# Attention with sinks and two MLPs on one core: another order of the attention pairs' steps in the opening stretch

## The chip, the cores and the metric

The kernel runs on one core of a Trainium2 chip. The metric is the device time of one execution in microseconds (us), taken as the median of several runs. The core has a matrix engine (TensorE, PE in the profile; its weight loads are PEld), VectorE (DVE), ScalarE (ACT), GpSimd (POOL) and SyncE (SP), whose queue issues the transfers from and to memory (DMA). Each engine executes its own instructions strictly in the order of the program, and waits for other engines by semaphores.

## The reference

Attention over 2 batches x 8 heads x 768 positions of 64 elements, where each position sees the last 128 positions and the first 4 (the sinks), and two MLPs one behind the other on the result (1536 tokens x 512, with 2048 inner features). All inputs are fp32.

```
scores = scale * q @ k.T
keep = (pos < n_sink) | ((rel >= 0) & (rel < window))
scores = where(keep, scores, -1e9);  scores -= max(scores)
a = exp(scores);  a = a / (sum(a) + 1e-9)
x = (a @ v)                                  # heads side by side: 1536 x 512
h = x @ w_in;   g = max(h, 0) + alpha * min(h, 0);   x = g @ w_out
h = x @ w2_in;  g = h - tanh(h);                     out = g @ w2_out
```

The weights are handed over as 64-bit numbers and converted to fp32 on the chip.

## The kernel before

**Pairs.** The attention is cut into 48 *pairs* of heads: a unit u is a batch and a block of 128 queries (12 units), and each unit has four pairs p; the pair's number is n = 4u + p. Two pairs share a *group* G = n // 2 of keys and queries. From the second block of a batch on, a pair's scores are 128 x 288 for each of its two heads (own block, previous block and 32 sink columns); in the first block they are 128 x 128.

**Steps of a pair.** `s_mm` (L244, L250): the scores on TensorE. From unit 1 on, keys and queries are split in a high and a low part, kept in `kq`, and three products (high-high, low-high, high-low) are added. `kq_hi` (L214, ScalarE) makes a group's high part, `kq_lo` (L217, VectorE) the low part as the difference, and `k_sinks` (L223) copies sink columns. `s_max` (L259, VectorE, an instruction and a short read of the accumulator for each head): mask and row maximum. `s_exp` (L268, ScalarE): exponential and its sum. `norm_sum` (L274 adds 1e-9 to the sums, L276 takes reciprocals) and `norm` (L283, one instruction per head), all VectorE. `sink_copy` (L292, VectorE, every second pair) gathers the sink columns. `t_mm` (L302, TensorE): transposes; `sink_mm` (L324) those of the sink columns. `t_ev` (L309) and `sink_ev` (L328) copy them out on ScalarE. `pv` (L341, L342, and L345 for sinks, TensorE): products with v. After every fourth pair `x_h` (L352, ScalarE) and `x_l` (L357, VectorE) store the unit's result as high and low part, the input of the first MLP.

**Stages.** The opening stretch is the loop of L531: 19 turns (`S_LEAD`), n = 0 to 18, one pair a turn, in which steps of neighbouring pairs are interleaved by hand: turn n makes the scores of pair n + 1, the maxima and exponentials of pair n, the norms and transposes of pair n - 1 and the products with v of pair n - 2. It also converts the first two weight tiles (L52 on ScalarE, then L54, L56, L58 and L60 on VectorE, one instruction a turn), splits one (L195, L200) and writes the masks (L488). The main loop (L621) then has 96 steps (2 MLPs x 3 token blocks x 16 feature tiles) of h products (L370), activation and output products (L422). Its first 29 pairs' worth of steps carry the remaining attention pairs, and its first 14 the rest of the first MLP's weight conversion.

**What sets the order.** The kernel is scheduled by hand: each engine's order is the order in which the code calls the steps. The order within one engine alone counts; that two calls for different engines change places has no effect. Loads of keys and queries (`load_qk`) are issued from SP four groups ahead, into six buffers.

Of the kernel before, what the change touches and what calls it, by code (L numbers as in the profile page):

```python
# [21 lines left out]
S_LEAD = 19  # L22
# [3 lines left out]
NU = B * NB  # L26
# [94 lines left out]
def fast_path(tc, qk, v, vsink, limits, w1i, w1o, alpha, w2i, w2o, out, outer):  # L121
# [3 lines left out]
    with ExitStack() as ctx:  # L125
# [79 lines left out]
        initial = [True]  # L205
# [7 lines left out]
        def kq_hi(G):  # L213
            nc.scalar.activation(out=kq_part(G, 0), in_=raws[G].rearrange("p c e t -> p c (e t)"), func=AF.Copy)  # L214

        def kq_lo(G):
            nc.vector.tensor_tensor(kq_part(G, 1), raws[G].rearrange("p c e t -> p c (e t)"), kq_part(G, 0), op=ALU.subtract)  # L217
# [60 lines left out]
        def norm(n):  # L278
            u, p, b, i, w = geom(n)
            G, hh = 2 * u + p // 2, 2 * (p % 2)  # L280
            for a in range(2):
                e = pq[G][:, hh + a, 0:w]
                nc.vector.tensor_scalar(e, e, sums[G][:, hh + a:hh + a + 1], None, op0=ALU.mult)  # L283
            if not initial[0]:
                sink_copy(n)

        def sink_copy(n):
            u, p, b, i, w = geom(n)
            G = 2 * u + p // 2
            if p % 2 == 1 and i >= 2:  # L290
                sks[G] = ap.tile([128, 4, SINK], F32, name="sk", bufs=1)
                nc.vector.tensor_copy(sks[G], pq[G][:, :, 128:160])  # L292
# [215 lines left out]
            if n == 4 * NB + 4:  # L508
                load_vs(1)

        def splits(n):

            todo = {0: (0,), 1: (2,), 2: (1,)}.get(n, (n // 2 + 2,) if n % 2 == 1 else ())
            for G in todo:
                if G < 2 * NU:
                    kq_hi(G)
                    kq_lo(G)
                    if G // 2 in (0, NB):
                        k_sinks(G)
# [11 lines left out]
        for n in range(S_LEAD):  # L531
            last = n == S_LEAD - 1
            a_loads(n)
            if n == 0:
                s_mm(0)
            if n >= 2:
                t_ev(n - 2)
            if not last:
                s_mm(n + 1)
            if n >= 1:  # L540
                norm_sum(n - 1, 0)
            s_max(n, 0)
            s_exp(n, 0)
            if n >= 1:
                norm_sum(n - 1, 1)
            s_max(n, 1)
            s_exp(n, 1)
            if n >= 2 and has_sinks(n - 2):
                sink_ev(n - 2)
            if n >= 5 and n % 4 == 2:  # L550
                x_l(n - 3)
            if n == 0:
                masks(0)
            if n >= 1:
                norm(n - 1)
            if n >= 2 and not last:
                pv(n - 2)
            if n >= 5 and n % 4 == 1:
                x_h(n - 2)
            splits(n)  # L560
            if n == 2:
                masks(1)
            if n == 3:
                load_w(0, 1)
            for f, at in CONV0:
                if n == at:
                    conv_start(0, f)
                if at < n < at + 5:
                    conv_step(0, f)
                if n == at + 4:  # L570
                    load_w(0, f + 2)
                if n == at + 6 and f == 0:
                    split_w(0, 0, 0, 0)
                    split_lo(0, 0, 0, 0)
            if n >= 1:
                sink_copy(n - 1)
                if not last:
                    t_mm(n - 1)
                    if has_sinks(n - 1):
                        sink_mm(n - 1, n + 1)  # L580
        initial[0] = False
        conv_start(0, len(CONV0))

# [37 lines left out]
        for g in range(N):  # L621
            m, c, f = steps[g]
            n = S_LEAD + g
            att = n < NPAIR + 3
            att_s = att and n < NPAIR
            back = steps[g - 1] if g else None
            first = g < NF
            conv = ahead = load = None
            L = len(CONV0)
            if first and g + L < NF:  # L630
                conv, ahead = (0, g + L), (0, g + L + 1) if g + L + 1 < NF else None
                load = (0, g + L + 2) if g + L + 2 < NF else None
            if g == CONV1 - 2:
                stage[1] = [ap.tile([128, 2048], I32, name="raw2", tag="kq", bufs=2) for _ in range(2)]
                load_w(1, 0)
                load_w(1, 1)
            if g == CONV1 - 1:
                ahead = (1, 0)
            conv1 = start.get(g, slow.get(g - 3))
            slow1 = next((slow[t] for t in range(g - 3, g + 1) if t in slow), None)  # L640
            if g in start:
                conv = (1, start[g])
            if g + 1 in start or g + 1 in slow:
                ahead = (1, start.get(g + 1, slow.get(g + 1)))
            if conv1 is not None and conv1 + 2 < NF:
                load = (1, conv1 + 2)
            if g == 2 * NF + 1:
                flag()
            if g == 2 * NF + 3:
                flag_rest()  # L650

            if att and n - 2 < NPAIR:
                t_mm(n - 2)
                t_ev(n - 2)
                if has_sinks(n - 2):
                    sink_mm(n - 2, n)
                    sink_ev(n - 2)
            if m == 0:
                if g + 1 < N:
                    split_w(*steps[g + 1], 0)  # L660
                if back:
                    split_w(*back, 1)
                if att_s:
                    a_loads(n)
                if att and n - 1 < NPAIR:
                    norm_sum(n - 1, 0)
                    norm_sum(n - 1, 1)
                    norm(n - 1)
                if conv:
                    conv_step(*conv)  # L670
                h_mm(m, c, f, 0, 2)
                if att_s:
                    s_mm(n)
                    for a in range(2):
                        s_max(n, a)
                        s_exp(n, a)
                h_mm(m, c, f, 2, 4)
                if back:
                    evac_mid(*back)
                    evac_hi(*back)  # L680
                    split_lo(*back, 1)
                if g + 1 < N:
                    split_lo(*steps[g + 1], 0)
                evac_first(m, c, f)
                if back:
                    evac_lo(*back)
                if conv:
                    conv_step(*conv, 3)
                if ahead:
                    conv_start(*ahead)  # L690
            elif m == 1:
                if back[0] == 0:
                    evac_mid(*back)
                    evac_hi(*back)
                    split_w(*back, 1)
                    split_lo(*back, 1)
                    evac_lo(*back)
                    split_w(*steps[g + 1], 0)
                    split_lo(*steps[g + 1], 0)
                if g != N - 1:  # L700
                    h_mm(m, c, f, 0, 4)
                if g == N - 2:
                    h_mm(*steps[g + 1], 0, 4)
                if g == N - 1:
                    out_mm(*steps[g - 3], 0, 4)
                if g < N - 2:
                    out_mm(*steps[g - 2], 0, 4)
                evac_first(m, c, f)
                if steps[g - 2][2] == NF - 1:
                    out_ev(*steps[g - 2][:2])  # L710
                evac_mid(m, c, f)
                if g + 2 < N:
                    split_w(*steps[g + 2], 0)
                split_w(m, c, f, 1)
                evac_hi(m, c, f)
                if g + 2 < N:
                    split_lo(*steps[g + 2], 0)
                split_lo(m, c, f, 1)
                evac_lo(m, c, f)
                if slow1 is not None:  # L720
                    conv_step(1, slow1)
                if ahead:
                    conv_start(*ahead)
            if m == 0 and g >= 2:
                out_mm(*steps[g - 2], 0, 4)
                if steps[g - 2][2] == NF - 1:
                    out_ev(*steps[g - 2][:2])
            if att:
                pv(n - 3)
                if n % 4 == 2:  # L730
                    x_h(n - 3)
                    x_l(n - 3)
                splits(n)
            if load:
                load_w(*load)
        for t in steps[N - 3:]:
# [179 lines left out]
```

## Time and profile before

| | |
|---|---|
| median of 3 runs | 702.11 us (701.14 to 704.3) |
| profiled execution | 701.61 us, its span 699.8 us |
| mean granted TensorE clock over the span | 0.981 of full speed |
| busy in the span: TensorE, VectorE, ScalarE | 655.1, 564.1, 433.3 us |
| busy tenths in the first five of 40 slices (17.5 us each) | TensorE 4 9 7 6 9, VectorE 5 6 7 7 8 |

The span is the time from the first to the last instruction; the profiled execution's own time is 1.8 us longer. Busy times are sums over one engine, idle times are given with what ended them ("releaser"), and the source line of each instruction is that of the kernel before. A matmul's end in the profile is modelled, so TensorE's rows are read best by their starts.

### The profile page before, as it was taken

To read this page: it belongs to the slowest core of one execution; us is meant where nothing else is said; L and a number is where in the kernel's file an instruction comes from. 1 tells how busy PE (TensorE), PEld (TensorE's weight loads), DVE (VectorE), ACT (ScalarE), POOL (GpSimd) and SP (SyncE) were. 2 spreads that over 40 slices of the span, in tenths; PEclk is the share of its full clock that TensorE was granted. 3 is DMA by queue.
4 is the path that set the end of the run, shared out by engine and by line. 5 is a ranking of instruction groups with operands and counts; after the bars stand their busy time and mean duration, and the time that the engine had idled before them with its cause. 6 is when DMAs were issued, how large, how long until landed. Compare 5 with 4: busy or idle time off the path is not lost.

```text
span 699.8 us, 9115 instructions
## 1 busy us (share of the span) xinstructions
PE 655.1 (94%) x3194; PEld 504.9 (72%) x3194; DVE 564.1 (81%) x1159; ACT 433.3 (62%) x872; POOL 1.1 (0%) x8
## 2 busy tenths in 40 slices
PE   4976989999999999999899999999999999999985
PEld 3654667766777777777688887777777777778763
DVE  5677899999967656658999987999888887887873
ACT  4756666657566565544646557777776777766653
POOL 0000000000000000000000000000000000000000
PEclk9987999999999999999999999999999999999999
DMA  3733244555010000113334330100010000100001
GB/s 107 225 116 111 76 142 153 183 169 170 12 46 2 15 16 1 59 64 120 121 125 170 127 121 1 60 1 0 1 60 1 1 0 1 60 1 1 0 1 65
DMA packets 27030, 47.35 MB, mean 68 GB/s; under 512 B 3168, under 2 KB 15456, under 8 KB 26976
## 3 DMA queue, kind: packets, MB, share of 16 engines
q1 hardware_dynamic: 26976, 46.68, 19.5%
q8 instruction: 27, 0.44, 0.3%
q14 instruction: 27, 0.22, 0.1%
HBM read 43.53 MB, written 3.15 MB: 67 GB/s over the span
## 4 chain that ended last, share of the span: by engine, by line
DVE 38%; PE 34%; ACT 20%; issue 4%; SPq 3%; DMA 1%; DVEq 0%; ACTq 0%
PE ps_h L370 13%; PE ps_o L422 13%; DVE u L106 5%; DVE g L109 4%; DVE g L108 4%; DVE t L107 4%; ACT mask L101 4%; ACT b L100 4%; ACT gh L401 4%; DVE wf L58 3%; ACT t L99 3%; ACT u L98 3%; DVE wl L200 3%; SPq L161 2%; DVE gl L406 2%
## 5 line engine op out<-in xcount | busy, mean ns | idle before, releaser
L370 PE MATMUL ps_h<-x,wh 128*128 128x512 f32 x384 | 127.6, 413 | 5.1 <-ACT t L377 3.6
L200 DVE TENSOR_TENSOR wl<-wf,wh 128x512 fp32r<-128x512 f32 x192 | 123.4, 683 | 10.7 <-ACT wh L195 10.5
L195 ACT ACTIVATE wh<-wf 128x512 fp32r<-128x512 f32 x192 | 111.2, 627 | 24.8 <-DVE sums L274 9.2
L370 PEld LDWEIGHTS ps_h<-x,wh 128*128 128x128 f32 x384 | 67.9, 190 | 24.1 <-ACT t L377 6.5
L401 ACT ACTIVATE gh<-g 128x512 fp32r<-128x512 f32 x48 | 30.4, 633 | 79.1 <-DVE g L109 79.1
L422 PE MATMUL ps_o<-wh,gh 128*128 128x512 f32 x192 | 74.8, 390 | 1.3 <-ACT gh L401 1.3
L370 PE MATMUL ps_h<-x,wl 128*128 128x512 f32 x192 | 76.0, 396 | 0.0
L268 ACT ACTIVATE pq<-pq,nm 128x288 f32<-128x288 f32 (+1 forms) x96 | 48.5, 506 | 43.5 <-DVE nm L259 43.2
L422 PE MATMUL ps_o<-gh,wh 128*128 128x512 f32 x192 | 75.4, 392 | 0.0
L422 PE MATMUL ps_o<-gl,wh 128*128 128x512 f32 x192 | 75.1, 391 | 0.0
L422 PE MATMUL ps_o<-gh,wl 128*128 128x512 f32 x192 | 75.0, 390 | 0.0
L422 PE MATMUL ps_o<-wh,gl 128*128 128x512 f32 x192 | 74.8, 390 | 0.0
L422 PE MATMUL ps_o<-wl,gh 128*128 128x512 f32 x192 | 74.7, 389 | 0.0
L401 ACT ACTIVATE gh<-t 128x512 fp32r<-128x512 f32 x48 | 30.0, 626 | 30.1 <-DVE t L389 30.1
L52 ACT ACTIVATE wf<-raw 128x1024 f32<-128x1024 f32 x32 | 36.7, 1146 | 15.2 <-DMA raw<-in_moe_w_out_dram 15.0
L309 ACT ACTIVATE pt<-ps_t 128x512 f32<-128x512 f32 (+1 forms) x39 | 21.8, 560 | 34.8 <-PE ps_t L302 34.7
L422 PEld LDWEIGHTS ps_o<-wh,gh 128*128 128x128 f32 x192 | 36.0, 188 | 9.2 <-ACT gh L401 1.8
L370 PEld LDWEIGHTS ps_h<-x,wl 128*128 128x128 f32 x192 | 36.4, 190 | 8.2
L422 PEld LDWEIGHTS ps_o<-gh,wh 128*128 128x128 f32 x192 | 36.3, 189 | 8.1 <-DVE y L433 0.4
L422 PEld LDWEIGHTS ps_o<-gl,wh 128*128 128x128 f32 x192 | 36.4, 189 | 7.7
L422 PEld LDWEIGHTS ps_o<-gh,wl 128*128 128x128 f32 x192 | 36.3, 189 | 7.7
L422 PEld LDWEIGHTS ps_o<-wh,gl 128*128 128x128 f32 x192 | 36.0, 188 | 7.9 <-DVE gl L406 0.4
(142 smaller groups left out, 1302.6 us busy)
## 6 DMA issues: line engine op xcount, KB each, us to landing
raw<-in_moe_w_in_dram SPq DMA_DIRECT2D x32, 512.0 KB, 3.4
raw<-in_moe_w_out_dram SPq DMA_DIRECT2D x32, 512.0 KB, 4.3
raw_qk<-in_qk_dram SPq DMA_DIRECT2D x96, 64.0 KB, 3.0
vt<-in_v_dram SPq DMA_DIRECT2D x12, 256.0 KB, 3.3
out_dram<-ob SPq DMA_DIRECT2D x2, 1024.0 KB, 4.3
out_dram<-ob SPq DMA_DIRECT2D x4, 256.0 KB, 3.3
vs<-in_vsink_dram SPq DMA_DIRECT2D x2, 256.0 KB, 3.4
ns_raw<-in_limits_dram SPq DMA_DIRECT2D x1, 2.0 KB, 2.5
```

Source lines behind the costliest of these rows:

```text
L52: nc.scalar.activation(out=dst, in_=hw.bitcast(F32), func=AF.Abs)
L100: nc.scalar.activation(out=b, in_=u, func=AF.Square, bias=shift)
L101: nc.scalar.activation(out=mask, in_=u, func=AF.Relu, bias=limit)
L106: nc.vector.scalar_tensor_tensor(u, h, P2, u, op0=ALU.mult, op1=ALU.mult)
L107: nc.vector.tensor_tensor(t, h, t, op=ALU.subtract)
L108: nc.vector.scalar_tensor_tensor(g, b, SQ_D, u, op0=ALU.add, op1=ALU.mult)
L195: nc.scalar.activation(out=hi, in_=src, func=AF.Copy)
L200: nc.vector.tensor_tensor(lo, wf[m, f][:, 512 * part:512 * part + 512], hi, op=ALU.subtract)
L268: nc.scalar.activation(out=e, in_=e, func=AF.Exp, scale=-1.0, bias=nm[:, 2 * n + a:2 * n + a + 1], accum_out=sums[G][:, hh:hh + 1])
L370: nc.tensor.matmul(h_ps[f], lhsT=l[:, w], rhs=x[:, r, kk, :], start=kk == 0 and e == 0, stop=kk == 3 and e == 2)
L401: nc.scalar.activation(out=gh, in_=mid[f], func=AF.Copy)
L422: nc.tensor.matmul(o, lhsT=l, rhs=r, start=f == 0 and e == 0, stop=f == NF - 1 and e == 2)
```

## The change

In each turn of the opening stretch:

- VectorE: both maxima of pair n first, then the sums, reciprocal and norms of pair n - 1 (before, sums and reciprocal stood between the maxima), the sink copy right behind the norms, and x_l behind the low parts.
- TensorE: the transposes of pair n - 1 (and of its sinks) ahead of the products with v of pair n - 2.
- ScalarE: the high part of a group one pair ahead of its low part; x_h behind the high part.
- The two calls that write masks are made at pairs 1 and 4 instead of 0 and 2.
- In the main loop high parts stay where they were, and low parts follow one step later.

```diff
-        def splits(n):
-
-            todo = {0: (0,), 1: (2,), 2: (1,)}.get(n, (n // 2 + 2,) if n % 2 == 1 else ())
-            for G in todo:
+        def splits_hi(n):
+
+            for G in {0: (0, 2), 1: (1,)}.get(n, (n // 2 + 2,) if n % 2 != (n < S_LEAD - 1) else ()):
                 if G < 2 * NU:
                     kq_hi(G)
+
+        def splits_lo(n):
+
+            early = n < S_LEAD
+            for G in {0: (0,), 1: (2,), 2: (1,)}.get(n, (n // 2 + 1 + early,) if n % 2 == early else ()):
+                if G < 2 * NU:
                     kq_lo(G)
                     if G // 2 in (0, NB):
                         k_sinks(G)
...
             if n == 0:
                 s_mm(0)
+            if not last:
+                s_mm(n + 1)
             if n >= 2:
                 t_ev(n - 2)
-            if not last:
-                s_mm(n + 1)
-            if n >= 1:
-                norm_sum(n - 1, 0)
             s_max(n, 0)
+            s_max(n, 1)
             s_exp(n, 0)
-            if n >= 1:
-                norm_sum(n - 1, 1)
-            s_max(n, 1)
             s_exp(n, 1)
             if n >= 2 and has_sinks(n - 2):
                 sink_ev(n - 2)
+            if n >= 1:
+                norm_sum(n - 1, 0)
+                norm_sum(n - 1, 1)
+                norm(n - 1)
+                sink_copy(n - 1)
+                if not last:
+                    t_mm(n - 1)
+                    if has_sinks(n - 1):
+                        sink_mm(n - 1, n + 1)
+            if n >= 2 and not last:
+                pv(n - 2)
+            splits_hi(n)
+            if n >= 5 and n % 4 == 1:
+                x_h(n - 2)
+            splits_lo(n)
             if n >= 5 and n % 4 == 2:
                 x_l(n - 3)
-            if n == 0:
+            if n == 1:
                 masks(0)
-            if n >= 1:
-                norm(n - 1)
-            if n >= 2 and not last:
-                pv(n - 2)
-            if n >= 5 and n % 4 == 1:
-                x_h(n - 2)
-            splits(n)
-            if n == 2:
+            if n == 4:
                 masks(1)
...
-            if n >= 1:
-                sink_copy(n - 1)
-                if not last:
-                    t_mm(n - 1)
-                    if has_sinks(n - 1):
-                        sink_mm(n - 1, n + 1)
...
+                    sink_copy(n - 1)
...
-                splits(n)
+                splits_hi(n)
+                splits_lo(n)
```

The order on VectorE in turn 9 of the opening stretch, before. `ISA` of L259 is a maximum and the read of its accumulator, `sums` are the sums of pair 8, `pq` its exponentials, `wf` a weight tile under conversion:

```order
L274 TENSOR_SCALAR sums<-sums 128x2
L259 ISA pq,nm<-ps_o,m_even 128x288
L259 ISA nm 128x1
L276 RECIPROCAL sums<-sums 128x2
L259 ISA pq,nm<-ps_o,m_even 128x288
L259 ISA nm 128x1
L283 TENSOR_SCALAR pq<-pq,sums 128x288
L283 TENSOR_SCALAR pq<-pq,sums 128x288
L217 TENSOR_TENSOR kq<-raw_qk,kq 128x2x256
L54 TENSOR_SCALAR wf<-wf 128x1024
```

And of the change, at the same place (lines behind the diff have moved by a few):

```order
L259 ISA pq,nm<-ps_o,m_even 128x288
L259 ISA nm 128x1
L259 ISA pq,nm<-ps_o,m_even 128x288
L259 ISA nm 128x1
L274 TENSOR_SCALAR sums<-sums 128x2
L276 RECIPROCAL sums<-sums 128x2
L283 TENSOR_SCALAR pq<-pq,sums 128x288 x2
L217 TENSOR_TENSOR kq<-raw_qk,kq 128x2x256
L54 TENSOR_SCALAR wf<-wf 128x1024
```

Sums and reciprocal have moved from between the maxima to behind them; the low part (L217) stands where it stood.

The order on ScalarE in turns 7 to 9, before; `pt` are copied transposes, `kq` a group's high part, and each L268 row with x2 is a pair's two exponentials:

```order
L309 ACTIVATE pt<-ps_t 128x512
L268 ACTIVATE pq,sums<-pq,nm 128x288 x2
L214 ACTIVATE kq<-raw_qk 128x2x256
L309 ACTIVATE pt<-ps_h 128x512
L268 ACTIVATE pq,sums<-pq,nm 128x288 x2
L52 ACTIVATE wf<-raw_89 128x1024
L309 ACTIVATE pt<-ps_t 128x512
L268 ACTIVATE pq,sums<-pq,nm 128x288 x2
L352 ACTIVATE x<-ps_v 128x4x128
L214 ACTIVATE kq<-raw_qk 128x2x256
```

And of the change, in the same turns and at the start of turn 10:

```order
L306 ACTIVATE pt<-ps_t 128x512
L268 ACTIVATE pq,sums<-pq,nm 128x288 x2
L306 ACTIVATE pt<-ps_h 128x512
L268 ACTIVATE pq,sums<-pq,nm 128x288 x2
L214 ACTIVATE kq<-raw_qk 128x2x256
L52 ACTIVATE wf<-raw_89 128x1024
L306 ACTIVATE pt<-ps_t 128x512
L268 ACTIVATE pq,sums<-pq,nm 128x288 x2
L349 ACTIVATE x<-ps_v 128x4x128
L306 ACTIVATE pt<-ps_h 128x512
```

The high part of turn 9's group has moved to the end of turn 8, behind that pair's exponentials; the one before had been made in turn 6.

The order on TensorE in turn 10, before: scores of pair 11, products with v of pair 8, transposes and sink transposes of pair 9, and the scores that follow in turn 11:

```order
L250 MATMUL ps_o<-kq 128x288 x6
L341 MATMUL ps_v<-pt,vt 64x128
L342 MATMUL ps_v<-pt,vt 64x128
L341 MATMUL ps_v<-pt,vt 64x128
L342 MATMUL ps_v<-pt,vt 64x128
L302 MATMUL ps_t<-ident,pq 128x128 x4
L324 MATMUL ps_o<-ident,sk 128x128
L250 MATMUL ps_o<-kq 128x288 x6
```

And of the change:

```order
L250 MATMUL ps_o<-kq 128x288 x6
L299 MATMUL ps_t<-ident,pq 128x128 x4
L321 MATMUL ps_o<-ident,sk 128x128
L338 MATMUL ps_v<-pt,vt 64x128
L339 MATMUL ps_v<-pt,vt 64x128
L338 MATMUL ps_v<-pt,vt 64x128
L339 MATMUL ps_v<-pt,vt 64x128
L250 MATMUL ps_o<-kq 128x288 x6
```

The products with v have moved behind the transposes, so that they stand directly ahead of the next scores.

## Rows read from the trace of the kernel before

**Rows 1.** Windows: stretch, length, busy time per engine, granted clock, DMA share, GB/s.
```profile
13.00:26.00 13.00, 10.40 (x57) 6.51 (x56) 9.49 (x52) 8.79 (x28) 0.00 (x0) 1.00 0.75 251
26.00:70.00 44.00, 32.18 (x228) 23.35 (x227) 32.53 (x123) 28.58 (x77) 0.00 (x0) 0.83 0.38 116
100.00:110.00 10.00, 10.00 (x62) 7.46 (x62) 9.83 (x20) 6.76 (x14) 0.00 (x0) 1.00 0.37 134
250.00:260.00 10.00, 10.00 (x63) 7.49 (x62) 5.38 (x15) 4.08 (x11) 0.00 (x0) 1.00 0.00 0
```

**Rows 2.** Waits from 0 to 13 us: total us, times, longest us.
```profile
DVE kq L217 <- ACT kq L214: 3.1, 2, 2.3
```

**Rows 3.** Waits from 13 to 30 us.
```profile
DVE kq L217 <- ACT kq L214: 4.9, 4, 1.8
```

**Rows 4.** Waits from 30 to 75 us.
```profile
DVE kq L217 <- ACT kq L214: 8.9, 5, 2.6
```

**Rows 5.** Timeline of VectorE at pair 18: start, duration, instruction, idle time before.
```profile
66.34 0.69 DVE L217 TENSOR_TENSOR kq<-raw_qk,kq 128x512 fp32r<-128x512 f32 x1 [2.63 <-ACT kq L214]
...
67.02 0.45 DVE L259 CUSTOM_DVE_ANT_0 pq<-ps_o,m_even 128x288 f32<-128x288 f32 x1
```

**Rows 6.** Timeline of VectorE in turn 9: sums and reciprocal between the maxima.
```profile
31.76 0.17 DVE L274 TENSOR_SCALAR sums<-sums 128x2 f32<-128x2 f32 x1 [0.47 <-ACT pq L268]
31.84 0.45 DVE L259 CUSTOM_DVE_ANT_0 pq<-ps_o,m_even 128x288 f32<-128x288 f32 x1
...
32.22 0.16 DVE L276 RECIPROCAL sums<-sums 128x2 f32<-128x2 f32 x1
32.29 0.43 DVE L259 CUSTOM_DVE_ANT_0 pq<-ps_o,m_even 128x288 f32<-128x288 f32 x1
...
32.66 0.64 DVE L283 TENSOR_SCALAR pq<-pq,sums 128x288 f32<-128x288 f32 x2
```

**Rows 7.** Timeline of VectorE in the main loop's first step: these instructions in a row.
```profile
69.25 0.16 DVE L274 TENSOR_SCALAR sums<-sums 128x2 f32<-128x2 f32 x1
69.45 0.17 DVE L276 RECIPROCAL sums<-sums 128x2 f32<-128x2 f32 x1
69.65 0.65 DVE L283 TENSOR_SCALAR pq<-pq,sums 128x288 f32<-128x288 f32 x2
70.21 0.69 DVE L54 TENSOR_SCALAR wf<-wf 128x1024 f32<-128x1024 f32 x1
73.22 0.46 DVE L259 CUSTOM_DVE_ANT_0 pq<-ps_s,m_even 128x288 f32<-128x288 f32 x1 [2.32 <-PE ps_t L250]
...
73.60 0.45 DVE L259 CUSTOM_DVE_ANT_0 pq<-ps_t,m_even 128x288 f32<-128x288 f32 x1
```

**Rows 8.** Timeline of VectorE: a sink copy right behind norms.
```profile
78.70 0.65 DVE L283 TENSOR_SCALAR pq<-pq,sums 128x288 f32<-128x288 f32 x2
79.39 0.23 DVE L292 COPY sk<-pq 128x128 f32<-128x128 f32 x1
```

**Rows 9.** Timeline of TensorE in turns 14 to 16, at the low clock.
```profile
55.36 0.48 PE L324 MATMUL ps_o<-ident,sk 128*128 128x128 f32 x1 [1.13 <-DVE sk L292]
55.76 1.09 PE L250 MATMUL ps_o<-kq 64*128 64x288 f32 x6
56.78 0.70 PE L341 MATMUL ps_v<-pt,vt 128*64 128x128 f32 x4
...
57.84 1.22 PE L345 MATMUL ps_v<-pts,vs 128*128 128x128 f32 x4
58.85 1.06 PE L302 MATMUL ps_h<-ident,pq 128*128 128x128 f32 x4
59.85 1.09 PE L250 MATMUL ps_o<-kq 64*128 64x288 f32 x6
```

**Rows 10.** Timeline in turn 14: a weight tile's high and low part.
```profile
53.22 0.61 ACT L195 ACTIVATE wh<-wf 128x512 fp32r<-128x512 f32 x1
...
53.87 0.69 DVE L200 TENSOR_TENSOR wl<-wf,wh 128x512 fp32r<-128x512 f32 x1
```

More of the change, by code (lines that the diff above doesn't have):

```diff
@@ L283, in norm @@
                 nc.vector.tensor_scalar(e, e, sums[G][:, hh + a:hh + a + 1], None, op0=ALU.mult)
-            if not initial[0]:
-                sink_copy(n)
         def sink_copy(n):
```

## The prediction

> **What bounds the kernel now.** I read the busy times by stretch first. From 26 to 70 us, the opening stretch's larger part, no engine is full: VectorE 32.53 of 44 us, TensorE 32.18, ScalarE 28.58 [rows 1]. From 100 to 110 us VectorE is busy 9.83 of 10, and at 250 to 260 us TensorE 10.00 of 10 [rows 1]. So the opening is held by waits, and two full engines follow it. An opening that ends earlier starts the rest earlier; nothing there gives it back, as long as the weight loads keep up (DMA share 0.37 at 100 us [rows 1]).
>
> Then the waits. One is far above the others on VectorE: L217, the low part of keys and queries, waits for L214, the high part, on ScalarE: 3.1 us in two waits before 13 us, 4.9 in four up to 30, 8.9 in five up to 75 [rows 2 to 4]. The reason is in the program: both parts stand in one step, L214 behind the two exponentials of the same pair, and L217 ahead of the next pair's maxima. VectorE stands, the next maxima are late, and so the next exponentials: at 66.34 the wait is 2.63 us, and the pair's maxima start right behind it, at 67.02 [rows 5]. I call the start of the first maximum of pair n D(n): D(9) is 31.84 [rows 6], D(18) is 67.02 [rows 5], D(19) is 73.22 [rows 7], so 3.91 us a pair from 9 to 18.
>
> **The change part by part.**
>
> *High parts a pair ahead.* L214 of a group moves one pair ahead of its L217. The next L217 then finds its operand done more than a pair earlier, and the waits from 13 us on go: 4.9 + 8.9 = 13.8 us. The two before 13 us stay: the longer (2.3 of the 3.1) ends when a load from memory lands, which nobody moves. The high part of group 2 now stands ahead of pair 1's exponentials while that load is under way. Their sums are asked for only behind group 2's low part, which has waited for the same load, so I take 0; the bound is the 2.3 of [rows 2] once more. Later loads are issued four pairs ahead of use, and are now needed three pairs ahead.
>
> *Maxima ahead of sums and norms.* The same seven instructions, in an order that costs more. Before, sums and reciprocal stand between the maxima: sums 31.76, maximum 31.84, reciprocal 32.22, maximum 32.29, norms 32.66, together 0.90 us [rows 6]. Afterwards the two maxima are neighbours (0.38 each, from 73.22 to 73.60 [rows 7]) and sums, reciprocal and norms stand in a row, each reading what the one ahead writes: 69.25, 69.45, 69.65, so 0.20 each where the interleaved ones took 0.07 [rows 6, 7]. 2 x 0.38 + 2 x 0.20 = 1.16, so 0.26 more a pair; 18 pairs, 4.7 us. What speaks against my price is the Trainium skill, VectorE: DVE Perf Modes, "The DRAIN you can't avoid": no next operation starts before the pipeline is empty, and a semaphore between two costs nothing extra. By it either order costs the same and this term is 0. The rows differ by 0.07 against 0.20, and I go by the rows.
>
> *The sink copy* (L292) now follows the norms at once instead of a conversion step. It starts 0.69 us behind the start of the two norms [rows 8]; an independent follower starts 0.56 behind (69.65 to 70.21 [rows 7]). 0.13 in five pairs: 0.65 us.
>
> *Transposes ahead of the products with v.* Per pair TensorE now does s(n+1), transposes (n-1), products (n-2). The transposes' input is ready 1.16 + 0.5 us behind D(n), so they no longer wait behind the products, but the products and the next s wait behind them. At the low clock level (1.2 GHz) the starts in [rows 9] give 1.02 for s (55.76 to 56.78), 1.06 for the products, 1.00 for the transposes (58.85 to 59.85), and every second pair another 1.01 for the sinks' products and 0.40 for their transposes: 6.16 + 1.41 over two pairs, 3.79 a pair. Without its waits VectorE comes to 1.16 + 0.56 = 1.72 a pair, plus 0.6 for a low part every second pair and the conversion instructions. Over pairs 9 to 18 that is 35.2 minus the 8.9 of waits plus 9 x 0.26 and the 0.65: 29.3 us, 3.25 a pair. At the high level (2.4 GHz) TensorE is the shorter of the two, at the low one not. Early on it counts most: from 13 to 26 us TensorE is already busy 10.40 of 13 [rows 1], and of what the four waits there are worth (4.9 - 9 x 0.26 = 2.6) anything from 0 to 2.6 can turn into waits for s. I take 1.4 lost, about the middle, since the reserve of 2.6 us is as large as the gain.
>
> *ScalarE.* x_h (L352) of every fourth pair waits for products that now stand behind the transposes, and holds the next exponentials; those sums are asked for a whole pair later, so 0. At pair 14 L195 now stands behind a high part and behind that x_h: before, L200 followed it by 0.65 us without a wait [rows 10]. Each of the two is about 0.6 long, like L195 itself [rows 10]; bounds 0 to 1.2, I take 0.6.
>
> *The masks* move from pairs 0 and 2 to 1 and 4; they are needed from pairs 4 and 8, the same count, no cost. *The join* to the first MLP step: VectorE waits 2.32 us at 73.22 for s products that stand behind six h products [rows 7], at a low clock. If TensorE comes in at the high level, its work takes about half as long; bounds 0 to 2.3, I take 0.9 gained. *In the MLP steps* low parts move to the next step; VectorE does the same work in a stretch where it is full: 0.
>
> Sum: 13.8 - 4.7 - 0.65 - 1.4 - 0.6 + 0.9 = 7.35 us earlier. The profiled execution took 701.61 us (span 699.8): 694.3. The median of the runs shown, 702.11, lies 0.5 above it, so I forecast 694.8.
>
> **The rivals.**
>
> A. *TensorE takes the place of the wait.* If it stays at the low level through the opening, pairs 9 to 18 cost 3.79 instead of 3.91: 9 x 0.12 = 1.1 us. Before pair 9 at most 2.6 comes. That is 3.7 in all if the join gives nothing: 698.4. For it: the mean granted clock from 26 to 70 us is only 0.83, and the low level there followed TensorE's idle times, as the 1.13 us wait before 55.36 [rows 1, 9]. Against it: the long idle times came with the VectorE waits that go, and an engine that is the bound has no idle time.
>
> B. *Regrouping costs nothing*, because the 0.20 of dependent neighbours is hidden by what follows, or was paid before as well: 4.7 more gained, 690.1. For it only that one dependent triple was read [rows 7]. The rule of the Trainium skill cited above (VectorE: DVE Perf Modes) would come to this.
>
> C. *Slower: transposes at the head of TensorE's line.* They wait for norms that start 1.16 us behind D(n). Before, the products with v filled that hole; now they stand behind it. If TensorE also stays low, it loses up to the 1.06 us of products [rows 9] in each of 13 pairs from 5 on: 13.8, against A's gain of 3.7, so 10 us slower at the worst (712); with two thirds of it 5.5 us, 707.6. It decides from the point where norms are later than the end of s(n+1) while TensorE, not VectorE, sets the pace. For it: transposes waited for norms before as well. Against it: where VectorE is late, TensorE has reserve by 3.25 against its high-level time, and where TensorE is the bound, the norms are early.
>
> D. *The change doesn't do what it says*, since high parts now wait for their loads: then the waits of 13.8 return on ScalarE and only the costs stay, 702.1 + 4.7 + 0.65 = 707.5. For it: a load did hold an early wait [rows 2]. Against: none of the later ones.
>
> **How the numbers follow.** Forecast 0.74 (own range 691.5 to 697.5, from the bounds of the join, pair 14 and the start), A 0.13, B 0.06, C 0.05, D 0.02. The range for 8 in 10 runs from 690.8 to 699.0: it takes in A, and leaves out B's lower half and the slower cases. 0.5%, about what a measurement tells from no change, is 3.5 us: faster means below 698.6. The forecast gives 0.72 of its 0.74, B 0.06, A about half: 0.84. The rest of A and the mild end of C are the same, 0.11; C and D slower, 0.05.
>
> **What would show it.** Waits of the low part for the high part between 13 and 75 us below 1 us in all; sums, reciprocal, norms 0.20 apart; the maxima of pair 19 at 65 to 67 us instead of 73.2; from 80 us on, every stage shifted by one and the same amount. TensorE's products nearly without gaps at the low level in the opening would show A, gaps ahead of the transposes with products ready behind them C. I am wrong if L217's wait goes and D(19) does not come at least 4 us earlier.

## The result, and the profile after

The changed kernel took 693.3 us (median of 4 runs, 693.13 to 693.4), the kernel before beside it 701.62 (4 runs): ratio 0.9877, 95% interval 0.9846 to 0.9908. The forecast was 694.8. Its profiled span is 691.4 us against 699.8, so 8.4 us shorter. One of e2's six executions further down (1265 us) and three of the kernel before beside e1 to e4 (912 to 2162 us) were far slower than all others of the same kernel; the ratios leave them out, and e2's median without its own is 706.83.

The windows of the changed kernel, to be laid beside [rows 1]: stretch, length, busy time of TensorE, its weight loads, VectorE, ScalarE and GpSimd, granted clock, DMA share, GB/s.

```profile
13.00:26.00 13.00, 11.71 (x64) 7.38 (x64) 12.19 (x62) 9.68 (x32) 0.00 (x0) 1.00 0.76 242
26.00:70.00 44.00, 34.56 (x267) 24.52 (x268) 39.42 (x129) 32.77 (x88) 0.00 (x0) 0.92 0.39 119
100.00:110.00 10.00, 9.76 (x53) 7.21 (x52) 9.79 (x20) 6.38 (x13) 0.00 (x0) 1.00 0.39 131
```

VectorE is now busy 39.42 of 44 us from 26 to 70 us where it was busy 32.53; from 100 to 110 us it is nearly full as before. What it waits for from 30 to 75 us (answers to [rows 4]: total, times, longest):

```profile
DVE wl L200 <- ACT wh L195: 1.2, 1, 1.2
DVE sums L274 <- ACT pq L268: 0.8, 1, 0.8
DVE pq L259 <- PE ps_t L250: 0.8, 1, 0.8
```

The wait of L217 for L214 is gone from this list; over the whole span its group reads so (instructions; busy time, mean ns; idle time before them):

```profile
L217 DVE TENSOR_TENSOR kq<-raw_qk,kq 128x512 fp32r<-128x512 f32 x24 | 16.4, 684 | 3.0 <-ACT kq L214 3.0
```

These 3.0 us are the two waits before 13 us, which were 3.1 before [rows 2]. VectorE in turn 9, the place of [rows 6], and its first maxima of pairs 18 and 19 with the sums between them, as in [rows 5, 7], from the changed kernel's timeline:

```profile
28.75 0.46 DVE L259 CUSTOM_DVE_ANT_0 pq<-ps_o,m_even 128x288 f32<-128x288 f32 x1
...
29.52 0.17 DVE L274 TENSOR_SCALAR sums<-sums 128x2 f32<-128x2 f32 x1
29.71 0.17 DVE L276 RECIPROCAL sums<-sums 128x2 f32<-128x2 f32 x1
29.91 0.65 DVE L283 TENSOR_SCALAR pq<-pq,sums 128x288 f32<-128x288 f32 x2
30.48 0.69 DVE L217 TENSOR_TENSOR kq<-raw_qk,kq 128x512 fp32r<-128x512 f32 x1
...
58.62 0.45 DVE L259 CUSTOM_DVE_ANT_0 pq<-ps_o,m_even 128x288 f32<-128x288 f32 x1
...
62.29 0.17 DVE L274 TENSOR_SCALAR sums<-sums 128x2 f32<-128x2 f32 x1 [0.82 <-ACT pq L268]
...
64.77 0.46 DVE L259 CUSTOM_DVE_ANT_0 pq<-ps_s,m_even 128x288 f32<-128x288 f32 x1 [0.78 <-PE ps_t L250]
```

The low part at 30.48 follows the norms without a wait. Sums, reciprocal and norms stand 0.20 us apart. D(18) is 58.62 against 67.02, so 8.40 earlier, D(19) 64.77 against 73.22, 8.45 earlier. From there on the lead stays as it is. The additions that end the first MLP's blocks (`y`, L433 before, L430 after; count, shortest/median/longest ns, first and last start) show it, first before, then after:

```profile
L433 DVE TENSOR_TENSOR y<-ps_o,y x12: 677/680/691, 211.0 to 425.5; 128x512 fp32r<-128x512 f32 x12
```

```profile
L430 DVE TENSOR_TENSOR y<-ps_o,y x12: 678/680/692, 202.6 to 416.9; 128x512 fp32r<-128x512 f32 x12
```

8.4 us at the first, 8.6 at the last, 8.4 at the end. What the opening wins here is what the kernel wins. In all the profiles of this document the time from D(19) to the end lies between 624.7 and 626.8 us, so this holds to within 2 us.

### The profile page after: what moved, and what is told of

Its sections match the earlier page's. It is cut to its first block, busy times and chain, and to the rows that moved or that the text cites. A ratio compares the mean times of both kernels' runs of the same rounds, so it can differ in the third digit from the quotient of the medians.

```text
span 691.4 us, 9101 instructions
## 1 busy us (share of the span) xinstructions
PE 649.9 (94%) x3194; PEld 500.6 (72%) x3194; DVE 567.5 (82%) x1159; ACT 432.9 (63%) x872; POOL 1.1 (0%) x8
## 4 chain that ended last, share of the span: by engine, by line
PE 38%; DVE 36%; ACT 19%; issue 3%; DMA 2%; SPq 1%; ACTq 0%; DVEq 0%
PE ps_o L419 14%; PE ps_h L367 14%; DVE u L106 5%; DVE g L109 4%; DVE g L108 4%; DVE t L107 4%; ACT mask L101 4%; ACT b L100 4%; ACT gh L398 3%; DVE wf L58 3%; ACT t L99 3%; ACT u L98 3%; DVE wl L200 2%; DVE wf L60 2%; PE ps_t L299 2%
## 5 line engine op out<-in xcount | busy, mean ns | idle before, releaser
L200 DVE TENSOR_TENSOR wl<-wf,wh 128x512 fp32r<-128x512 f32 x192 | 123.3, 682 | 11.9 <-ACT wh L195 11.7
L195 ACT ACTIVATE wh<-wf 128x512 fp32r<-128x512 f32 x192 | 111.3, 627 | 24.6 <-DVE sums L274 9.3
L268 ACT ACTIVATE pq<-pq,nm 128x288 f32<-128x288 f32 (+1 forms) x96 | 48.4, 506 | 35.9 <-DVE nm L259 35.9
L419 PEld LDWEIGHTS ps_o<-wl,gh 128*128 128x128 f32 x192 | 36.2, 188 | 7.6
```

The costliest lines, as they stand in the source:

```text
L195: nc.scalar.activation(out=hi, in_=src, func=AF.Copy)
L200: nc.vector.tensor_tensor(lo, wf[m, f][:, 512 * part:512 * part + 512], hi, op=ALU.subtract)
L268: nc.scalar.activation(out=e, in_=e, func=AF.Exp, scale=-1.0, bias=nm[:, 2 * n + a:2 * n + a + 1], accum_out=sums[G][:, hh:hh + 1])
L419: nc.tensor.matmul(o, lhsT=l, rhs=r, start=f == 0 and e == 0, stop=f == NF - 1 and e == 2)
```

## The experiments

D(9), D(18) and D(19) are starts of first maxima in each kernel's one profiled execution. The median is of its timed runs, the ratio against the kernel before on the same chip. e1 to e4, e5 to e8 and e9 to e12 ran together, each group on a chip of its own.

| kernel | D(9) | D(18) | D(19) | span | median | ratio (95%) |
|---|---|---|---|---|---|---|
| before | 31.84 | 67.02 | 73.22 | 699.8 | | |
| the change | 28.75 | 58.62 | 64.77 | 691.4 | 693.3 | 0.9877 (0.9846-0.9908) |
| e1_high_ahead | 29.21 | 56.47 | 61.93 | 686.9 | 691.34 | 0.9858 (0.9837-0.9879) |
| e2_without_high | 33.42 | 72.59 | 79.52 | 705.2 | 706.98 | 1.007 (1.005-1.009) |
| e3_products_first | 28.16 | 58.10 | 64.17 | 690.6 | 690.72 | 0.984 (0.9819-0.986) |
| e4_interleaved | 29.43 | 58.02 | 63.91 | 690.7 | 691.85 | 0.9854 (0.9832-0.9875) |
| e5_change_again | 29.55 | 59.07 | 64.96 | 689.7 | 691.51 | 0.9869 (0.9847-0.9892) |
| e6_high_ahead_again | 29.63 | 57.52 | 62.98 | 688.1 | 691.66 | 0.9869 (0.9843-0.9895) |
| e7_high_ahead_wl_later | 28.68 | 55.37 | 60.64 | 686.2 | 688.68 | 0.983 (0.9808-0.9853) |
| e8_change_wl_later | 29.03 | 57.30 | 63.18 | 689.7 | 691.79 | 0.9867 (0.9845-0.989) |
| e9_old_maxima_first_half | 29.32 | 57.58 | 63.47 | 690.3 | 692.01 | 0.9862 (0.9844-0.988) |
| e10_old_maxima_second_half | 28.94 | 55.16 | 60.98 | 687.7 | 688.38 | 0.9811 (0.9794-0.9829) |
| e11_transposes_first | 30.61 | 57.25 | 64.45 | 691.0 | 692.80 | 0.9864 (0.9841-0.9887) |
| e12_high_ahead_wl_again | 29.81 | 56.42 | 61.70 | 688.5 | 688.87 | 0.9824 (0.9802-0.9845) |

Three kernels were profiled twice: the change and e5, e1 and e6, e7 and e12. Between the two profiles of one kernel D(9) lies 0.42 to 1.13 us apart, D(18) 0.45 to 1.05, and the time from D(9) to D(18) only 0.08 to 0.63. So less than about 1 us at D(18) tells two kernels apart no more than chance does.

**Which part brings the gain?** My theory was that the high parts alone do, and that the rest costs. The rival was that TensorE's new order, transposes first, is what gains.

e1 is the kernel before with the high parts moved and nothing else in the opening (with the new `splits_hi` and `splits_lo` the main loop's low parts come one step later, as in the change):

```diff
-            splits(n)
+            splits_hi(n)
+            splits_lo(n)
```

> The kernel before with one part of the change alone: high parts a pair ahead of low parts; maxima, sums, transposes and products in the old order. Theory (VectorE sets the opening's pace, and its waits for the high parts are what goes; regrouping only costs): the waits of 13.8 us go, and 4.7 us of regrouping and 0.65 us of sink copies aren't paid, so at least as fast as the whole change: 689 to 693 us. Rival (TensorE's order: transposes behind the products with v hold the pairs): less than half of the change's 8.3 us, 697.5 or more, with the waits replaced by waits of VectorE for scores.

e2 is the changed kernel with the high parts back beside their low parts:

```diff
-            splits_hi(n)
             if n >= 5 and n % 4 == 1:
                 x_h(n - 2)
-            splits_lo(n)
+            splits(n)
```

> The changed kernel with high parts back in the same step as their low parts; all of the regrouping and the transposes ahead stay. Theory: VectorE waits for L214 again, the more so as maxima come first only by 0.26 us; 700 to 704 us, no gain. Rival (TensorE's order is what gains): 694 to 697.

e1 gives the whole gain: D(18) is 10.55 us earlier than before, more than the change's 8.40, and it stands ahead of the main loop. e2 is slower than before, which neither side expected. L217 there waits 11.4 us from 30 to 75 us where it waited 8.9 [rows 4]:

```profile
DVE kq L217 <- ACT kq L214: 11.4, 6, 3.5
```

Why one of these waits is longer stands in ScalarE's rows in turn 9 (start, duration, idle time before):

```profile
37.60 0.60 ACT L349 ACTIVATE x<-ps_v 128x512 fp32r<-128x512 f32 x1 [1.45 <-PE ps_v L339]
38.09 0.62 ACT L214 ACTIVATE kq<-raw_qk 128x512 fp32r<-128x512 f32 x1
```

The high part stands behind x_h, and x_h waits 1.45 us for products that now stand behind the transposes; before, x_h started there, at 34.18, without a wait. So the rest of the change, taken without the high parts, only costs, and this part of the cost falls away when the high part leaves that place.

**Which of the rest costs?** e3 is the changed kernel with products ahead of transposes again, e4 has sums and reciprocal back among the maxima and their reads, but with the reciprocal still directly ahead of the norms.

```diff
-                if not last:
-                    t_mm(n - 1)
-                    if has_sinks(n - 1):
-                        sink_mm(n - 1, n + 1)
             if n >= 2 and not last:
                 pv(n - 2)
+            if n >= 1 and not last:
+                t_mm(n - 1)
+                if has_sinks(n - 1):
+                    sink_mm(n - 1, n + 1)
```

> The changed kernel with TensorE's old order: products with v ahead of the transposes. Theory (VectorE sets the pace, TensorE has reserve): 693 to 695, the same as the change within its interval, with waits of TensorE ahead of the transposes as in the kernel before but shorter. Rival (transposes first are needed): 697.5 or more.

```diff
             s_max(n, 0)
+            if n >= 1:
+                norm_sum(n - 1, 0)
             s_max(n, 1)
+            if n >= 1:
+                norm_sum(n - 1, 1)
...
-                norm_sum(n - 1, 0)
-                norm_sum(n - 1, 1)
```

> The changed kernel with the sums behind the first maximum and the reciprocal behind the second, so that no two neighbours depend on each other; all else of the change stays. Theory (0.20 for each of two dependent neighbours against 0.07): about 0.26 less in each of 18 pairs, 4.7 us if VectorE sets the pace throughout, less where it waits for TensorE at the start: 688.5 to 691.5. Rival B (regrouping costs nothing): 693.3. Second rival: the sums are asked for earlier and wait for the exponentials, so only a part, 692 to 693.

Both differ from the change by less than a microsecond at D(18) and D(19), and their intervals overlap its own, so neither is told from it. e3's 690.72 us lies below the 693 to 695 I expected. e4 came out slower than I expected, where its second rival was nearer: with the reciprocal still directly ahead of the norms, only half of the price is given back (1.03 us from the first maximum to the norms in turn 9, 29.43 to 30.46, against 1.16 in the change and 0.90 before), and its sums wait longer for exponentials, 1.3 us from 13 to 75 us against 0.8.

**Is e1 faster than the change?** A direct comparison, both unchanged: 

> The changed kernel once more, for a direct comparison with the kernel that makes high parts a pair ahead and changes nothing else. Theory (all the gain is the high parts', and regrouping with the transposes' move costs what the maxima of pair 19 showed, 2.8 us): median 692 to 694, 1.5 to 3 us slower than that kernel. Rival (the two are alike, and what the high parts bring is limited by the stages behind the opening): both within 1 us of each other.

> The kernel before with the high parts a pair ahead alone, beside the changed kernel on the same chip. Theory: median 690 to 691.5, the maxima of pair 19 at 61.5 to 62.5 us. Rival: 692 to 694, like the changed kernel.

The medians are alike (691.51 and 691.66), as the rival said, although D(19) is 1.98 us earlier in e6 (62.98, a little later than expected) and the profiled span 1.6 shorter. Single runs of each scatter over 3 to 4 us (690.61 to 693.62, 689.31 to 693.48), so a difference of 2 us is not resolved by five of them.

**The wait at pair 14.** In the changed kernel L200 waits for L195, and TensorE then has nothing to do. VectorE, then TensorE, then windows of the changed kernel:

```profile
48.18 0.69 DVE L200 TENSOR_TENSOR wl<-wf,wh 128x512 fp32r<-128x512 f32 x1 [1.17 <-ACT wh L195]
```

```profile
47.32 0.66 PE L250 MATMUL ps_o<-kq 64*128 64x288 f32 x6
51.06 1.09 PE L299 MATMUL ps_h<-ident,pq 128*128 128x128 f32 x4 [3.08 <-DVE pq L283]
```

```profile
49.00:50.00 1.00, 0.00 (x0) 0.00 (x0) 1.00 (x4) 0.11 (x1) 0.00 (x0) 1.00 0.20 59
50.00:51.00 1.00, 0.00 (x0) 0.00 (x0) 0.93 (x6) 1.00 (x5) 0.00 (x0) 0.86 0.13 36
51.00:54.00 3.00, 2.94 (x16) 2.31 (x16) 2.93 (x10) 1.45 (x6) 0.00 (x0) 0.50 0.00 0
54.00:57.00 3.00, 3.00 (x17) 2.17 (x18) 2.72 (x7) 1.60 (x4) 0.00 (x0) 0.50 0.00 0
57.00:58.00 1.00, 1.00 (x14) 0.68 (x10) 0.93 (x6) 1.00 (x5) 0.00 (x0) 0.72 0.88 225
```

TensorE idles 3.08 us, and then its granted clock is 0.50 (1.2 GHz) until 57 us. e7 (on e1) and e8 (on the change) make the low part a turn later:

```diff
                     split_w(0, 0, 0, 0)
+                if n == at + 7 and f == 0:
                     split_lo(0, 0, 0, 0)
```

> High parts a pair ahead, and the low part of the first weight tile (L200) made one turn later than its high part (L195), so that VectorE does not wait for ScalarE at pair 14. Theory (the wait of 1.3 us holds the next maxima, and TensorE's idle time behind it lets its clock fall): the wait gone, the maxima of pair 19 at 60 to 61 us, no stretch at the low clock from 50 us on, median 688.5 to 690. Rival (another wait takes its place, since ScalarE's exponentials of the pair are as late as L195): pair 19 at 61.5 to 62.5, 690 to 692.

> The changed kernel with the low part of the first weight tile one turn later than its high part. Theory: the wait of 1.2 us at 48 us gone, TensorE's clock not falling at 51 us, the maxima of pair 19 at 62 to 63.5 us instead of 64.8, median 690.5 to 692. Rival (the wait moves to the next exponentials or transposes): pair 19 within 0.6 us of 64.8, 692.5 to 694.

The wait and the low stretch at 51 us are gone in both; e7's profile has a low stretch from 31 to 35 us instead, e6's had one at 44 to 47 as well. TensorE in e8, at the same place:

```profile
49.47 0.63 PE L299 MATMUL ps_h<-ident,pq 128*128 128x128 f32 x4 [1.22 <-DVE pq L283]
```

D(19) comes 2.34 us earlier in e7 than in e6 and 1.78 earlier in e8 than in e5. Both are where the theory put them, but part of that stands at D(9) already, ahead of this edit. Counted from D(9) it is 1.39 and 1.26 us, about the wait itself. The low stretch cost little: from the first maximum of pair 15 to D(18) the change takes 9.23 us with it, e5 8.88 with it, and e8 9.50 without it, of which 0.60 is the low part that was moved there. That makes 0.3 us at most. e7's median followed (688.68 against 691.66, though the intervals still overlap), e8's did not come below the change's (691.79 against 691.51), so for the change this gain is shown in the opening only.

**Where is the order of the maxima paid?** Two kernels on e8, with the old order of VectorE in turns 1 to 8 alone (e9) and in turns 9 to 18 alone (e10). This is e9; in e10 the first line reads `old = n >= 9`.

```diff
+            old = 1 <= n < 9
+            if old:
+                norm_sum(n - 1, 0)
             s_max(n, 0)
+            if old:
+                norm_sum(n - 1, 1)
             s_max(n, 1)
...
-                norm_sum(n - 1, 0)
-                norm_sum(n - 1, 1)
+                if not old:
+                    norm_sum(n - 1, 0)
+                    norm_sum(n - 1, 1)
```

> The changed kernel with the low weight part a turn later, and in turns 1 to 8 alone VectorE's old order again (sums and reciprocal between the maxima). Theory (in these turns TensorE sets the pace, and the 0.26 us a turn of the regrouped order lie beside it): the maxima of pair 18 within 0.6 us of 57.30, the time as that of the same kernel without this edit, 690.5 to 692.5. Rival (the price is paid in each turn, as the prediction had it): pair 18 about 2.1 us earlier, at 55 to 55.6, time 688.5 to 690.5.

> The same kernel with VectorE's old order in turns 9 to 18 alone. Theory (there VectorE sets the pace, so each turn gives the 0.24 to 0.26 us back): the maxima of pair 18 at 54.7 to 55.3 instead of 57.30, time 688 to 690. Rival (the cost from pair 9 on lies with the transposes' place, not with the order of maxima and norms): pair 18 within 0.6 us of 57.30, 690.5 to 692.5.

Both came out as the theory had them. e9 leaves D(18) at 57.58 (57.30 in e8), e10 takes it to 55.16. From D(9) to D(18) e8 needs 28.27 us, e9 28.26, e10 26.22: 2.05 us in nine turns, 0.23 a turn, all three with the granted clock at 1.00 throughout. The intervals of e9 and e10 do not meet. Turn 12 on VectorE, in e10 and then in e8:

```profile
38.02 0.16 DVE L274 TENSOR_SCALAR sums<-sums 128x2 f32<-128x2 f32 x1
38.09 0.45 DVE L259 CUSTOM_DVE_ANT_0 pq<-ps_o,m_odd 128x288 f32<-128x288 f32 x1
...
38.47 0.16 DVE L276 RECIPROCAL sums<-sums 128x2 f32<-128x2 f32 x1
38.54 0.43 DVE L259 CUSTOM_DVE_ANT_0 pq<-ps_o,m_odd 128x288 f32<-128x288 f32 x1
...
38.90 0.64 DVE L283 TENSOR_SCALAR pq<-pq,sums 128x288 f32<-128x288 f32 x2
```

```profile
38.59 0.45 DVE L259 CUSTOM_DVE_ANT_0 pq<-ps_o,m_odd 128x288 f32<-128x288 f32 x1
...
38.97 0.45 DVE L259 CUSTOM_DVE_ANT_0 pq<-ps_o,m_odd 128x288 f32<-128x288 f32 x1
...
39.34 0.16 DVE L274 TENSOR_SCALAR sums<-sums 128x2 f32<-128x2 f32 x1
39.54 0.17 DVE L276 RECIPROCAL sums<-sums 128x2 f32<-128x2 f32 x1
39.74 0.65 DVE L283 TENSOR_SCALAR pq<-pq,sums 128x288 f32<-128x288 f32 x2
```

The same instructions take 0.88 us to the norms in e10 and 1.15 in e8. From start to start, a maximum, which needs nothing of the sums or the reciprocal ahead of it, follows them after 0.07 us; the reciprocal follows the sums, and the norms the reciprocal, after 0.20. e10 also has the lowest ratio measured: 0.9811 (0.9794 to 0.9829), below both intervals of the change. e7 and e12, which are one kernel, come as near to it as can be told (0.983 and 0.9824), and e3's interval touches it.

Where e9's saving goes is in VectorE's rows. At pair 6 its maxima are 0.42 us ahead of e8's (20.94 against 21.36). Then it waits for exponentials of pair 6 and, at pair 9, for scores:

```profile
24.77 0.17 DVE L274 TENSOR_SCALAR sums<-sums 128x2 f32<-128x2 f32 x1 [0.82 <-ACT pq L268]
...
29.32 0.46 DVE L259 CUSTOM_DVE_ANT_0 pq<-ps_o,m_even 128x288 f32<-128x288 f32 x1 [0.96 <-PE ps_o L250]
```

**The transposes' place.** e11 is e7 with the transposes ahead of the products (and the sink copy behind the norms, since the sinks' transposes read it), e12 is e7 again.

```diff
                 norm(n - 1)
+                sink_copy(n - 1)
+                if not last:
+                    t_mm(n - 1)
+                    if has_sinks(n - 1):
+                        sink_mm(n - 1, n + 1)
             if n >= 2 and not last:
                 pv(n - 2)
...
-            if n >= 1:
-                sink_copy(n - 1)
-                if not last:
-                    t_mm(n - 1)
-                    if has_sinks(n - 1):
-                        sink_mm(n - 1, n + 1)
```

> High parts a pair ahead with the low weight part a turn later, and the transposes ahead of the products with v, with the sink copy right behind the norms; maxima, sums and norms stay in the old order. Theory (the transposes' place costs little, as products first and transposes first gave 64.17 and 64.77 in the changed kernel): the maxima of pair 18 within 0.8 us of the 55.37 without this edit, time within 1 us of it. Rival (it is the transposes' place that costs): pair 18 at 56.8 to 57.5, time 2 us more.

> High parts a pair ahead with the low weight part a turn later, once more, beside the three others. Theory (the shorter opening reaches the end): 688 to 690, the maxima of pair 19 at 60.3 to 61. Rival (the earlier median was chance): 690.5 to 692.

e12 repeats e7's time, though with D(19) at 61.70, later than expected. On the transposes my theory missed: e11 takes 692.80 us, e12 688.87, and their intervals only just meet. The steady turns cost nothing (D(9) to D(18): 26.64 in e11, 26.61 in e12). The time goes at both ends: 0.80 us at D(9), which is no more than e7 and e12 differ, and 1.92 more from D(18) to D(19) (7.20 against 5.28). TensorE, the windows and VectorE of e11 at the join:

```profile
60.17 0.63 PE L302 MATMUL ps_t<-ident,pq 128*128 128x128 f32 x4 [1.78 <-DVE pq L283]
```

```profile
62.00:64.00 2.00, 2.00 (x10) 1.22 (x8) 0.29 (x1) 0.73 (x3) 0.00 (x0) 0.50 0.00 0
```

```profile
64.45 0.46 DVE L259 CUSTOM_DVE_ANT_0 pq<-ps_s,m_even 128x288 f32<-128x288 f32 x1 [2.17 <-PE ps_t L250]
```

Behind the last products TensorE is idle for 1.78 us, then runs at 0.50, and VectorE waits 2.17 us for the scores of pair 19. In e12 the idle time is 1.35 us, the clock stays at 1.00 there, and the wait is 0.86. Whether the place of the transposes brings this each time stays open. One profile of each shows it, and in the changed kernel the same swap (e3) moved D(19) by only 0.60.

## Why the prediction was right, step by step

The mechanism, the sign and the size were right; some terms were not, and that their errors partly cancel is luck.

- *13.8 us of waits go*: right. 16.9 us of waits of L217 in the span became 3.0, all of it before 13 us, where nothing was expected to change. (The loads have more room than I said: by the code a group's high part comes five turns behind the issue of its load before and four after, not four and three.) The high parts alone bring D(18) 10.55 us earlier (9.50 in e6); the rest of the 13.8 comes back as waits of the sums for the exponentials (2.9 us in e1 from 13 to 30 us, 0.4 before) and as the wait at pair 14 (1.3 in e1).
- *Regrouping costs 4.7*: the step that failed is "18 pairs". The price of one turn was nearly right (0.26 from [rows 6, 7]; 0.23 by e8 and e10). But it is paid only in the nine turns from 9 on, where VectorE sets the pace: 2.05 us. In turns 1 to 8 undoing it brings nothing at D(9) (e9). The busy times don't tell why: from 13 to 26 us both TensorE (11.71 of 13) and VectorE (12.19) are nearly full. TensorE's rows do: from the first of the two rows below, of the changed kernel, to the second, none is shown with idle time ahead of it, while VectorE, given its time back in e9, waits. What the old order can have brought there is the 0.21 us by which e9's TensorE is ahead of e8's (scores at 25.63 against 25.84); it is lost again because e9's TensorE keeps the durations of the low level longer (products of 0.70 us at 27.69, in e8 of 0.45 at 27.74).

```profile
14.29 0.69 PE L299 MATMUL ps_t<-ident,pq 128*128 128x128 f32 x2 [2.73 <-DVE pq L283]
...
31.34 0.45 PE L338 MATMUL ps_v<-pt,vt 128*64 128x128 f32 x4 [0.26 <-ACT pt L306]
```

- *1.4 us lost to TensorE at the start*: this took the same stretch a second time. Up to pair 9 my terms made 4.9 - 2.34 - 1.4 = 1.2 us; measured were 3.09 (2.29 in e5). A cost on VectorE and a bound on TensorE lie beside each other, and I had added them. TensorE also left its low level earlier in this profile, at 26.88 us instead of 30.96; in e5, the same kernel, it was at about 28.4, and D(9) 0.80 later, so part of the 3.09 is chance. The profile's granted clock says 1.00 there all the time, so the level is inferred from the durations (six score products in 1.09 us, as at the low clock in [rows 9], or in 0.66). Before the change, then after it:

```profile
29.94 1.09 PE L250 MATMUL ps_o<-kq 64*128 64x288 f32 x6
30.96 0.45 PE L341 MATMUL ps_v<-pt,vt 128*64 128x128 f32 x4
```

```profile
25.86 1.09 PE L250 MATMUL ps_o<-kq 64*128 64x288 f32 x6
26.88 0.66 PE L299 MATMUL ps_h<-ident,pq 128*128 128x128 f32 x4
```

- *Pair 14 costs 0.6*: 1.17 us, the upper bound, and TensorE's idle time with it. L195 stands behind the high part and x_h, as said, but x_h itself, at 45.00, waits 1.77 us for products behind the transposes.
- *x_h costs 0, since its sums are asked for a pair later*: wrong at the last turn. ScalarE of the changed kernel there:

```profile
60.14 0.60 ACT L349 ACTIVATE x<-ps_v 128x512 fp32r<-128x512 f32 x1 [1.83 <-PE ps_v L342]
...
61.11 0.54 ACT L268 ACTIVATE pq<-pq,nm 128x288 f32<-128x288 f32 x1
```

  x_h holds pair 18's exponentials, and the sums at 62.29 wait 0.82 us for them. The main loop asks for a pair's sums ahead of the next pair's maxima, not behind them.
- *The join gains 0.9*: it gained 0.05 (D(18) to D(19): 6.20 before, 6.15 after). The wait did fall from 2.32 us [rows 7] to 0.78, but the 0.82 just named took its place, with the sums and reciprocal of pair 17: 0.40 us behind pair 18's maxima now (59.37 to 59.77), where they had stood ahead of and between them (66.95 and 67.39).

Sum: 7.35 predicted at D(19), 8.45 measured, so D(19) came at 64.77, a little ahead of the 65 to 67 us that were to show the mechanism. Regrouping, sink copy and start were charged 4.7 + 0.65 + 1.4 = 6.75; what is left for them at D(18) is 13.8 - 1.17 - 8.40 = 4.2, so 2.5 less. No run tests the sink copy's 0.65 by itself. Pair 14 and the join came out 0.6 and 0.85 worse.

Of the rivals, A did not come: the mean granted clock from 26 to 70 us is 0.92 instead of 0.83. That this clock is itself a cause of the gain no run tests alone; the low stretch behind pair 14, which cost 0.3 us at most, speaks against much of it. B was right for the first eight turns, for another reason than its own. The Trainium skill, VectorE: DVE Perf Modes, "The DRAIN you can't avoid", has no next operation start before the pipeline is empty, and by that sentence e8 and e10 would not differ; but the rows differ by 0.07 against 0.20 and the time by the intervals above, and the measurement decides. The same paragraph excepts a next operation that is not held, which I left out of the prediction; a maximum that starts 0.07 us behind sums of 0.16 us agrees with the exception. C's mechanism is seen, if small: in e11 at the join, in the changed kernel in x_h's waits for products behind the transposes. D did not come, since the waits went. Its sum is near that of e2, where the waits stay and the costs are added (707.5 worked out, 706.98 measured), but by chance: e2 has 1.4 us more of waits (18.3 instead of 16.9) and fewer turns that pay.

## What to carry to other kernels

Where one engine makes a value and another uses it in the same step of a hand-ordered pipeline, move the producer a step ahead: the waits on the user's queue are the most that the stage can win (here 13.8 us of waits brought 9.5 to 10.6 by that move alone), and here that lead reached the end one to one, to within 2 us. Price an order of instructions by what lies between neighbours (dependent ones here cost three times as much), but charge it only in those turns in which that engine sets the pace. Before moving work ahead on a third engine, look at who waits for what it is moved past.

## What the runs showed of the hardware that was not expected

TensorE's clock rises and falls at different times in the same program. Of e7 and e12, which are one kernel, the first runs its transposes at the high level's duration at 24.19 (four in 0.66 us, against 1.06 at the low clock in [rows 9]), the second its products still at the low one's at 26.34 (0.70, as in [rows 9]):

```profile
24.19 0.66 PE L302 MATMUL ps_t<-ident,pq 128*128 128x128 f32 x4
```

```profile
26.34 0.70 PE L341 MATMUL ps_v<-pt,vt 128*64 128x128 f32 x4
```

D(9) differs by 1.13 us with it. Far behind the opening, too, the change's first profile has low stretches that its second (e5) lacks, here the first and then the second:

```profile
150.00:155.00 5.00, 3.61 (x15) 2.75 (x15) 4.90 (x13) 3.77 (x10) 0.00 (x0) 0.81 0.40 134
...
665.00:670.00 5.00, 2.91 (x9) 1.98 (x10) 3.94 (x7) 3.32 (x7) 0.00 (x0) 0.85 0.01 3
```

```profile
150.00:155.00 5.00, 4.39 (x22) 3.42 (x22) 4.90 (x13) 2.99 (x7) 0.00 (x0) 1.00 0.37 141
...
665.00:670.00 5.00, 2.98 (x12) 2.16 (x13) 3.86 (x7) 3.30 (x6) 0.00 (x0) 1.00 0.01 3
```

From D(19) to the end the first takes 626.6 us, the second 624.7. That is the scatter in which a difference of 2 us in the opening is lost when only medians of five runs are compared, and why D(18), D(19) and the time between D(9) and D(18) told more here than the total times.
